# Three input buffers per chunk, wider zero products, and a rolled-up general path in a gated-recurrence and MLP kernel

## The chip, the cores and the metric

One core of one Trainium2 chip. The time is device microseconds of one execution; the kernel runs as one launch, and the host only lays the inputs out and the output back.

## The reference

Every head of `q`, `k`, `v`, `f_logit` (4 batches, 8 heads, 768 steps, 48 wide) runs a gated linear recurrence; the result, as 3072 tokens of 384, goes through a two-layer MLP (384 to 2048 to 384) with the activation h*tanh(softplus(h)). All is float32.

```python
f = 1.0 / (1.0 + np.exp(-f_logit))
for t in range(S):
    state = f[:, :, t, :, None] * state + np.einsum('bhd,bhe->bhde', k[:, :, t], v[:, :, t])
    y[:, :, t] = np.einsum('bhd,bhde->bhe', q[:, :, t], state)
...
x = np.ascontiguousarray(attn_out.transpose(0, 2, 1, 3)).reshape(B * S, H * D)
h = x @ w_in
sp = np.where(h > 20.0, h, np.log1p(np.exp(np.minimum(h, 20.0))))
g = h * np.tanh(sp)
return (g @ w_out).astype(np.float32)
```

## The kernel before

The recurrence is cut into 24 chunks (6 stretches of 128 steps for each of 4 batches). For a chunk n, `load` brings the inputs `l` (gate logits), `k`, `q`, `v` (256 KB each) into one of two buffers (`n % 2`); `prep` forms the cumulated gates on ScalarE (lines 358, 359, 374, 375), VectorE (357) and TensorE (362, chunks 0 to 7) and multiplies `k` and `q` by them (277, on VectorE or GpSimd); `attn0` makes the scores (398) and masks them (404); `attn1` transposes `k` (423, copied by 426); `attn2` forms the state's update (440; `mid` at 453 or 456, `tmp` at 458); `attn3` makes the chunk's output (474, 486), splits it into a high and a low part in `xt` (512, 517 or 519), moves the state on (502), and, when the last chunk of a group of four is done, spreads some rows of `xt` over the others by DMA (525).

Each group of four chunks is 512 tokens of the MLP, worked off as 16 units (one for each 128 hidden columns j): `moe_in` (219, nine products of 512 columns), the activation `mish` (229 to 237, over ScalarE, VectorE and GpSimd), `moe_out` (242, nine products). The first two groups take turns: j 0 to 7 of group 0, j 0 to 7 of group 1, then j 8 to 15 of each. Before the first unit of a j, `split_w(j)` loads 768 KB of weights (`raw`, two buffers, line 320) and makes a high and a low part: ScalarE 322 and 329, VectorE 324, 325, 327 and 330. Results leave through `ob` (585 to 591) by DMA (592).

All this is recorded first, as steps with a cost, and `Plan.order` sets each engine's order by list scheduling with those costs and with the buffers as dependences; the program is then issued in that order. All DMAs are issued by SyncE's queue (SP). Where the plan has TensorE idle before the first `moe_out`, `Plan.issue` puts products on zeros (`idle`, line 310) into the gap.

At the end, `ends` (the chunks' last decays) is tested (620 to 625) into `flag`; all five engines load `flag` (633) and jump over the body of `tc.If` (634), the general path for decays that the fast path can't take. It isn't run with these inputs, but its code lies between the branch and the end of the program.

Of the kernel before, what the change touches and what calls it, by code (L numbers as in the profile page):

```python
# [9 lines left out]
F32 = mybir.dt.float32  # L10
# [29 lines left out]
LEAD = [(-4, 4), (24, 32)]  # L40
LAG = 2


class Plan:
# [130 lines left out]
def recurrence_moe_kernel(  # L175
# [36 lines left out]
    state0 = ctile([P, P], F32, "state0")  # L212


    def moe_in(h, xt, j):
# [24 lines left out]
    def moe_out(o, m, gh, gl, j, first, last):  # L240
# [6 lines left out]
    with tc.tile_pool(name="work", bufs=1) as pool, tc.tile_pool(  # L247
# [5 lines left out]
        l_, k_, q_ = (ring(nm, 2, [P, NP, C]) for nm in "lkq")  # L253
        v_ = ring("v", 2, [P, H * 64])
# [54 lines left out]
        def idle():  # L309
            nc.tensor.matmul(zeros[:, 0:P], state0[:, 0:P], state0[:, 0:P], start=True, stop=True)  # L310
# [23 lines left out]
        def load(n, parts):  # L334
            i = n % 2
# [8 lines left out]
        def prep(n, parts):  # L344
            i = n % 2
# [40 lines left out]
        def attn0(n, parts):  # L386

            k, q = k_[n % 2], q_[n % 2]
# [18 lines left out]
            def reads(s):  # L407
                return pairs(("k", n % 2), range(s, s + st)) + pairs(("q", n % 2), range(s, s + st))
# [8 lines left out]
        def attn1(n):  # L417
            b, key = at1.rearrange("p (a c) -> p a c", a=NP), ("at", 2)
            k = k_[n % 2]
# [5 lines left out]
            add("pe", 400, transposes, pairs(("k", n % 2)), [key])  # L425
            add("act", T_ACT(GT, True), lambda: nc.scalar.activation(kt_s, b, AF.Copy), [key], ["kt"])

        def attn2(n):
            last = n >= NCH - B
            st, ks = state[:, n % B], ("st", n % B)  # L430
            v = v_[n % 2]
# [13 lines left out]
            if n >= GC:  # L445
                scores, mask, reads, writes = late[n]
                add("pe", 1208, lambda: [update(), scores()], ["kt", ("v", n % 2)] + reads,
                    list(dict.fromkeys(keys[: 2 - last] + writes)))
                mask()
            else:  # L450
                add("pe", 745, update, ["kt", ("v", n % 2)], keys[: 2 - last])
# [8 lines left out]
        def attn3(n):  # L460
            i = n % 2
# [99 lines left out]

        def out_unit(u):
# [18 lines left out]
            if last:  # L581
                dst = halves[g] if j < NF - 1 else out[:, g * GT : (g + 1) * GT]
                for m in range(NK):
# [6 lines left out]
                    else:  # L590
                        add("dve", T_DVE(GT), lambda m=m: nc.vector.tensor_copy(ob_[m], o_[m]), [("o", m)], pairs(("ob", m)))
# [4 lines left out]
        for u in range(len(units) + LAG):  # L596
# [22 lines left out]
        ok, oks = at1[0:1, 0:1], state.rearrange("p b a c -> p (b a c)")[:, : NCH * NP]  # L619
        add("dve", 119, lambda: nc.vector.tensor_scalar(  # L620
            oks, ends.rearrange("p n a b -> p (n a b)"), DEC_OK, None, ALU.is_ge),
            [x for n in range(NCH) for x in pairs(("end", n))], [("st", b) for b in range(B)])
        add("dve", 169, lambda: nc.vector.tensor_reduce(okc, oks, mybir.AxisListType.X, ALU.add), [("st", 0)], ["okc"])
        add("pe", 26, lambda: nc.tensor.matmul(ok, ones, okc, start=True, stop=True), ["okc"], [("at", 2)])
        add("dve", 65, lambda: nc.vector.tensor_copy(flag, ok), [("at", 2)], ["flag"])
# [8 lines left out]
    with tc.If(good < total):  # L634
        xs = dram.tile([DM, NT], F32, tag="xs", name="xs")
        with tc.tile_pool(name="slow", bufs=1) as pool, tc.tile_pool(
# [9 lines left out]
            with tc.For_i(0, B, 1) as b:  # L646
                for p in range(NP):
                    f, k, q = (st([P, NCB, C], nm) for nm in ("sf", "sk", "sq"))
                    for dst, src in ((f, fl), (k, kk), (q, qq)):
                        nc.sync.dma_start(  # L650
                            dst, src.rearrange("(c b) p a t -> p a c b t", b=B)[:, p, :, ds(b, 1), :]
                            .rearrange("p c b t -> p c (b t)"),
# [3 lines left out]
                    with tc.For_i(0, D, 1) as e:  # L656
                        v = st([P, S], "sv")
                        for i in range(2):
                            nc.sync.dma_start(
                                v[64 * i : 64 * i + 64, :],  # L660
                                vt[ds(b, 1), 2 * p + i, ds(e, 1), :]
                                .rearrange("a c t -> (a c) t")
# [12 lines left out]
                        for i in range(2):  # L675
                            nc.sync.dma_start(
# [101 lines left out]
```

## Time and profile before

| | us |
|---|---|
| median of 3 runs | 529.99 |
| lowest, highest | 527.87, 534.02 |
| profiled execution, time | 533.71 |
| profiled execution, span (first to last instruction) | 531.9 |
| TensorE, busy share of the span | 96% |
| VectorE, busy share | 70% |
| ScalarE, busy share | 78% |
| GpSimd, busy share | 30% |

Busy time of TensorE counts the products on zeros too, and its matmuls overlap, so its share doesn't tell how much of the span is useful work.

### The profile page before, as it was taken

To read this page: it belongs to the slowest core of one execution; us is meant where nothing else is said; L and a number is where in the kernel's file an instruction comes from. 1 tells how busy PE (TensorE), PEld (TensorE's weight loads), DVE (VectorE), ACT (ScalarE), POOL (GpSimd) and SP (SyncE) were. 2 spreads that over 40 slices of the span, in tenths; PEclk is the share of its full clock that TensorE was granted. 3 is DMA by queue.
4 is the path that set the end of the run, shared out by engine and by line. 5 is a ranking of instruction groups with operands and counts; after the bars stand their busy time and mean duration, and the time that the engine had idled before them with its cause. 6 is when DMAs were issued, how large, how long until landed. Compare 5 with 4: busy or idle time off the path is not lost.

```text
span 531.9 us, 13034 instructions
## 1 busy us (share of the span) xinstructions
PE 512.8 (96%) x5358; PEld 409.7 (77%) x5358; DVE 369.7 (70%) x588; ACT 415.4 (78%) x731; POOL 157.4 (30%) x134
## 2 busy tenths in 40 slices
PE   8899999999899999999999999999999999999993
PEld 7678777777677777787787777787787787778882
DVE  4478999899897887866576777567657563645451
ACT  6777988888789798878778788878878776778770
POOL 2231442334132322412322332413131222132320
PEclk9899999999899999999999999999999999999998
DMA  7597554344230443321212330112221000000001
GB/s 263 208 293 257 167 173 131 88 154 140 98 99 21 143 138 110 118 64 60 62 41 90 101 100 25 58 41 90 61 79 41 4 0 33 26 33 1 1 1 67
DMA packets 22629, 48.91 MB, mean 92 GB/s; under 512 B 2656, under 2 KB 3808, under 8 KB 22560
## 3 DMA queue, kind: packets, MB, share of 16 engines
q1 hardware_dynamic: 22560, 47.98, 28.1%
q8 instruction: 44, 0.72, 0.6%
q14 instruction: 25, 0.20, 0.1%
HBM read 39.32 MB, written 6.29 MB: 86 GB/s over the span
## 4 chain that ended last, share of the span: by engine, by line
PE 82%; DVE 7%; DMA 3%; ACT 3%; issue 2%; SPq 0%; POOL 0%; DVEq 0%; ACTq 0%
PE h L219 35%; PE o L242 34%; PE at L486 2%; PE at L474 2%; PE at L440 2%; DMA xt<-xt 2%; PE at L423 2%; PE at L398 2%; DVE wt L325 1%; DMA raw<-ww 1%; DVE g L232 1%; DVE wl L330 1%; DVE n L231 1%; PE at L362 1%; PE o L310 1%
## 5 line engine op out<-in xcount | busy, mean ns | idle before, releaser
L237 POOL TENSOR_TENSOR gl<-g,gh 128x512 fp32r<-128x512 f32 x96 | 129.9, 1356 | 302.5 <-ACT gh L236 274.3
L219 PE MATMUL h<-xt,wh 128*128 128x512 f32 x576 | 185.9, 404 | 3.4 <-DVE g L235 2.4
L219 PEld LDWEIGHTS h<-xt,wh 128*128 128x128 f32 x576 | 105.7, 189 | 31.1 <-DVE g L235 4.8
L242 PE MATMUL o<-gh,wh 128*128 128x512 f32 x288 | 116.5, 405 | 0.0
L219 PE MATMUL h<-xt,wl 128*128 128x512 f32 x288 | 114.2, 397 | 0.0
L242 PE MATMUL o<-gl,wh 128*128 128x512 f32 x288 | 113.7, 395 | 0.0
L242 PE MATMUL o<-gh,wl 128*128 128x512 f32 x288 | 113.7, 395 | 0.0
L231 DVE SCALAR_TENSOR_TENSOR n<-n 128x512 f32<-128x512 f32 x96 | 71.1, 740 | 54.7 <-ACT n L230 54.5
L235 DVE TENSOR_TENSOR g<-g,h 128x512 f32<-128x512 f32 x96 | 65.3, 682 | 42.1 <-ACT h L234 41.7
L229 ACT ACTIVATE n<-h,hcap 128x512 f32<-128x512 f32 x96 | 65.7, 685 | 31.5 <-PE h L219 30.8
L233 ACT ACTIVATE h<-n,two 128x512 f32<-128x512 f32 x96 | 65.8, 686 | 29.3 <-DVE g L232 29.3
L236 ACT ACTIVATE gh<-g 128x512 fp32r<-128x512 f32 x96 | 60.1, 627 | 16.1 <-DVE g L235 14.1
L232 DVE TENSOR_TENSOR g<-h,n 128x512 f32<-128x512 f32 x96 | 66.1, 689 | 8.9 <-POOL gl L237 1.1
L230 ACT ACTIVATE n<-n,hcap 128x512 f32<-128x512 f32 x96 | 69.2, 721 | 2.1
L219 PEld LDWEIGHTS h<-xt,wl 128*128 128x128 f32 x288 | 54.4, 189 | 13.3
L242 PEld LDWEIGHTS o<-gh,wh 128*128 128x128 f32 x288 | 54.0, 188 | 13.5 <-ACT ob L588 0.3
L242 PEld LDWEIGHTS o<-gl,wh 128*128 128x128 f32 x288 | 54.0, 187 | 13.3
L242 PEld LDWEIGHTS o<-gh,wl 128*128 128x128 f32 x288 | 54.1, 188 | 11.8
L234 ACT ACTIVATE h<-h 128x512 f32<-128x512 f32 x96 | 55.9, 582 | 1.8
L519 DVE TENSOR_TENSOR xt<-at,xt 128x256 fp32r<-128x256 f32 x40 | 15.9, 418 | 13.4 <-ACT xt L512 13.2
L502 POOL TENSOR_TENSOR state<-tmp,ends 128x256 f32<-128x256 f32 x20 | 16.7, 834 | 28.6 <-PE at L474 22.1
L404 DVE TENSOR_TENSOR a<-at,causal 128x256 f32<-128x256 f32 x44 | 17.7, 418 | 7.4 <-PE at L398 7.3
(102 smaller groups left out, 525.2 us busy)
## 6 DMA issues: line engine op xcount, KB each, us to landing
raw<-ww SPq DMA_DIRECT2D x16, 768.0 KB, 5.2
v<-vn SPq DMA_DIRECT2D x24, 256.0 KB, 3.7
k<-kk SPq DMA_DIRECT2D x23, 256.0 KB, 3.1
q<-qq SPq DMA_DIRECT2D x23, 256.0 KB, 2.9
out<-ob SPq DMA_DIRECT2D x18, 256.0 KB, 2.3
l<-fl SPq DMA_DIRECT2D x16, 256.0 KB, 2.7
xt<-xt SPq DMA_DIRECT2D x15, 128.0 KB, 2.1
l<-ft SPq DMA_DIRECT2D x7, 256.0 KB, 3.8
```

Of the source, the lines that this page charges most:

```text
L219: nc.tensor.matmul(h, w[:, j, a * P : (a + 1) * P], xt[:, x, a, :], start=(n == 0), stop=(n == 3 * NK - 1))
L229: ("act", T_ACT(GT, True, 1), 0, lambda: nc.scalar.activation(u, h, AF.Relu, bias=hcap, scale=-1.0)),
L230: ("act", T_ACT(GT, False, 1), 0, lambda: nc.scalar.activation(u, u, AF.Exp, bias=hcap, scale=-1.0)),
L231: ("dve", T_DVE(GT), 1, lambda: nc.vector.scalar_tensor_tensor(n, u, 2.0, u, ALU.add, ALU.mult)),
L232: ("dve", T_DVE(GT), 0, lambda: nc.vector.tensor_tensor(g, h, n, ALU.mult)),
L233: ("act", T_ACT(GT, False, 1), 0, lambda: nc.scalar.activation(h, n, AF.Ln, bias=two)),
L234: ("act", T_ACT(GT, True), 0, lambda: nc.scalar.activation(h, h, AF.Exp, scale=-1.0)),
L235: ("dve", T_DVE(GT), 0, lambda: nc.vector.tensor_tensor(g, g, h, ALU.mult)),
L236: ("act", T_ACT(GT), 0, lambda: nc.scalar.activation(gh, g, AF.Copy)),
L237: ("pool", T_POOL(GT), 1, lambda: nc.gpsimd.tensor_tensor(gl, g, gh.bitcast(F32), ALU.subtract)),
L242: nc.tensor.matmul(o, w[:, j, m * P : (m + 1) * P], x, start=(first and i == 0), stop=(last and i == 2))
L404: add("dve", T_DVE(NP * CH), lambda e=e: nc.vector.tensor_tensor(a_[e], sc[e], causal[:, None, :].broadcast_to([P, NP, CH]), ALU.mult), [k ...
```

## The change

Four edits. The rings of `l`, `k`, `q` and `v` get three buffers (`NR`) for two, which also removes dependences from the plan; the scheduler then writes another order for every engine. The zero product is 256 columns wide for 128, and is put in at twice the pitch, in gaps of over 527 ns of the plan for 313; the order holds 66 of the narrow ones before and 27 of the wide ones now. The test of `ends` is recorded ahead of the last unit's output, and the last copies into `ob` read `flag`, so that the test can't be put behind them. The general path becomes nested loops with fewer and wider DMAs, most of them issued by ScalarE's queue. Counted in the two built programs, waits included and a matrix product as its weight load and its multiply, the jump over it spans 746 instructions of TensorE before and 161 now, 284 and 163 of ScalarE, 250 and 139 of VectorE, 332 and 179 of SP, 175 and 125 of GpSimd. The scratch for dynamic DMAs is set to 1024. In the changed file everything behind line 41 stands one line lower, and more from line 560 on.

```diff
+NR = 3
...
-                    while at + 313.0 < self.start[i]:
+                    while at + 527.0 < self.start[i]:
                         self.idle()
-                        at += 213.0 if at > 6500.0 else 426.0
+                        at += 427.0 if at > 6500.0 else 853.0
...
-        l_, k_, q_ = (ring(nm, 2, [P, NP, C]) for nm in "lkq")
-        v_ = ring("v", 2, [P, H * 64])
+        l_, k_, q_ = (ring(nm, NR, [P, NP, C]) for nm in "lkq")
+        v_ = ring("v", NR, [P, H * 64])
...
-            nc.tensor.matmul(zeros[:, 0:P], state0[:, 0:P], state0[:, 0:P], start=True, stop=True)
+            nc.tensor.matmul(zeros[:, : 2 * P], state0[:, 0:P], state0, start=True, stop=True)
...
-            i = n % 2
+            i = n % NR
...
+        def check():
+            ok, oks = at1[0:1, 0:1], state.rearrange("p b a c -> p (b a c)")[:, : NCH * NP]
+            add("dve", 119, lambda: nc.vector.tensor_scalar(
...
+            add("dve", 65, lambda: nc.vector.tensor_copy(flag, ok), [("at", 2)], ["flag"])
...
-                        add("dve", T_DVE(GT), lambda m=m: nc.vector.tensor_copy(ob_[m], o_[m]), [("o", m)], pairs(("ob", m)))
+                        add("dve", T_DVE(GT), lambda m=m: nc.vector.tensor_copy(ob_[m], o_[m]),
+                            [("o", m)] + ["flag"] * (u == len(units) - 1), pairs(("ob", m)))
...
+            if u == len(units):
+                check()
             if u >= LAG:
                 out_unit(u - LAG)
...
-                for p in range(NP):
+                with tc.For_i(0, NP, 1) as p:
...
-                        nc.sync.dma_start(
+                        nc.scalar.dma_start(
...
-                for j in range(NF):
-                    moe_in(h, xt, j)
+                with tc.For_i(0, NF, 1) as j:
+                    for w, whole in zip(wj, (wh, wl)):
+                        nc.vector.tensor_copy(w, whole[:, ds(j, 1), :].bitcast(F32))
+                    moe_in(h, xt, 0, *(w[:, :, : NK * P] for w in wj))
...
-    nc = bacc.Bacc("TRN2", target_bir_lowering=False, num_devices=1)
+    nc = bacc.Bacc("TRN2", target_bir_lowering=False, num_devices=1, dynamic_dma_scratch_size=1024)
```

Three places in the order. First SP, at the start, behind the loads of chunks 0 and 1. Names are buffers: `l0` is the first buffer of `l`, `raw0` the first of the weights. Before the change SP issues here:

```order
L339 DMA l0_81<-ft 128x512
L320 DMA raw0_112<-ww 128x1536
L320 DMA raw1_113<-ww 128x1536
L339 DMA l1_82<-ft 128x512
L339 DMA k0_83<-kk 128x512
L339 DMA q0_85<-qq 128x512
L342 DMA v0_87<-vn 128x512
```

The same place now:

```order
L340 DMA l0_81<-ft 128x512
L340 DMA k2_86<-kk 128x512
L340 DMA q2_89<-qq 128x512
L343 DMA v2_92<-vn 128x512
L340 DMA l1_82<-ft 128x512
L321 DMA raw0_116<-ww 128x1536
L340 DMA k0_84<-kk 128x512
L321 DMA raw1_117<-ww 128x1536
```

The first two weight loads moved behind the inputs of chunk 2, which no longer wait for a buffer of chunk 0.

Second ScalarE, between chunk 2's `mid` and the output of chunk 3. Before the change, up to chunk 3's `mid` and the rest of chunk 2's output (`wt` holds weights on their way to `wh`):

```order
L453 ACTIVATE mid0_95<-at2_118 128x256
L358 ACTIVATE l0_81<-l0_81 128x512
L329 ACTIVATE wh_61<-wt0_114 128x768
L359 ACTIVATE l0_81<-l0_81,ones_69 128x512
L426 ACTIVATE kt0_89<-at2_118 128x512
L512 ACTIVATE xt0_97<-o1_122 128x2x128
L512 ACTIVATE xt0_97<-o0_121 128x2x128
L517 ACTIVATE xt0_97<-o1_122 128x2x128
L322 ACTIVATE wt0_114<-raw0_112 128x768
L453 ACTIVATE mid0_95<-at2_118 128x256
L329 ACTIVATE wh_61<-wt1_115 128x768
L517 ACTIVATE xt0_97<-o0_121 128x2x128
```

The same place now:

```order
L454 ACTIVATE mid0_99<-at2_122 128x256
L323 ACTIVATE wt0_118<-raw0_116 128x768
L323 ACTIVATE wt1_119<-raw1_117 128x768
L513 ACTIVATE xt0_101<-o1_126 128x2x128
L427 ACTIVATE kt0_93<-at2_122 128x512
L513 ACTIVATE xt0_101<-o0_125 128x2x128
L518 ACTIVATE xt0_101<-o1_126 128x2x128
L518 ACTIVATE xt0_101<-o0_125 128x2x128
L454 ACTIVATE mid0_99<-at2_122 128x256
L330 ACTIVATE wh_61<-wt0_118 128x768
```

Before, the copy of the third weight load (322) stood ahead of chunk 3's `mid` and the first two had been copied earlier; now the first two stand here, and the third behind the output of chunk 3.

Third SP, at the end, from the last group's output on. Before the change SP issues the three output DMAs first:

```order
L592 DMA out<-ob_109 128x512
L592 DMA out<-ob_110 128x512
L592 DMA out<-ob_111 128x512
L633 TENSOR_LOAD flag
L633 ISA x2
L634 COMPARE_AND_BRANCH
```

The same place now:

```order
L639 TENSOR_LOAD flag
L639 ISA x2
L604 DMA out<-ob_113 128x512
L604 DMA out<-ob_114 128x512
L604 DMA out<-ob_115 128x512
L640 COMPARE_AND_BRANCH
```

The load of `flag` and its two checks moved ahead of the last three output DMAs.

## Rows read from the trace of the kernel before

**Rows 1.** The page: its span, and the chain of waits that ended last, by engine.

```profile
span 531.9 us, 13034 instructions
...
PE 82%; DVE 7%; DMA 3%; ACT 3%; issue 2%; SPq 0%; POOL 0%; DVEq 0%; ACTq 0%
```

**Rows 2.** Busy time by stretch: start and end, length, then busy us (and instructions) of PE, PEld, DVE, ACT and POOL, the granted clock, the DMA share and GB/s. The row for 44.4 to 160 is of VectorE alone.

```profile
20.00:44.40 24.40, 22.40 (x493) 19.42 (x491) 18.93 (x30) 17.72 (x39) 6.79 (x6) 0.95 0.74 238
60.00:130.00 70.00, 68.96 (x734) 54.16 (x735) 65.17 (x94) 60.46 (x102) 27.34 (x20) 1.00 0.43 138
130.00:139.00 9.00, 6.65 (x21) 4.71 (x20) 8.35 (x10) 5.97 (x9) 2.63 (x2) 0.81 0.29 89
160.00:442.80 282.80, 282.80 (x3166) 224.11 (x3165) 198.70 (x330) 228.34 (x408) 82.99 (x68) 1.00 0.22 68
...
44.40:160.00 115.60, 107.13 (x152) 0.99 0.44 142
```

**Rows 3.** The timeline of the start: start and length in us, engine, line, operation, tiles, count, and in brackets the idle time before it and what ended it.

```profile
18.09 0.57 PE L440 MATMUL at<-v,kt 64*64 64x64 f32 x22 [2.57 <-issue]
19.83 0.55 DVE L324 TENSOR_SCALAR wt<-wt 128x768 int32<-128x768 int32 x1
26.15 0.38 ACT L453 ACTIVATE mid<-at 128x256 f32<-128x256 f32 x1
31.54 0.89 ACT L322 ACTIVATE wt<-raw 128x768 f32<-128x768 f32 x1 [1.53 <-DMA raw<-ww]
32.33 0.37 ACT L453 ACTIVATE mid<-at 128x256 f32<-128x256 f32 x1
37.37 0.54 SPq L320 DMA_DIRECT2D raw<-ww  x1
38.44 1.48 SPq L525 DMA_DIRECT2D xt<-xt  x2
44.39 0.73 PE L219 MATMUL h<-xt,wh 128*128 128x512 f32 x2 [0.86 <-DMA xt<-xt]
```

**Rows 4.** What VectorE waited for from 40 to 160 us: line, releaser, us in total, times, longest.

```profile
DVE g L235 <- ACT h L234: 2.9, 3, 1.8
DVE xt L519 <- ACT xt L512: 2.0, 3, 0.8
DVE wt L324 <- ACT wt L322: 1.2, 2, 1.0
DVE n L231 <- ACT n L230: 1.0, 2, 0.5
```

**Rows 5.** The products on zeros, all of them (duration min/median/max in ns, first and last start), and, from the timeline of TensorE, the stop near 133 us and the products behind it.

```profile
L310 PE MATMUL o<-state x132: 271/275/580, 1.1 to 55.1; 128*128 128x128 f32 x132
...
132.60 0.40 PE L219 MATMUL h<-xt,wl 128*128 128x512 f32 x1
135.13 1.22 PE L219 MATMUL h<-xt,wh 128*128 128x512 f32 x2 [2.13 <-DVE g L235]
...
138.85 0.39 PE L242 MATMUL o<-gh,wh 128*128 128x512 f32 x1
```

**Rows 6.** The end, from the timeline.

```profile
522.09 1.74 SPq L592 DMA_DIRECT2D out<-ob  x3
522.77 0.69 DVE L591 COPY ob<-o 128x512 f32<-128x512 f32 x1 [0.71 <-PE o L242]
523.38 0.14 DVE L625 CAST flag<-at 1x1 int32<-1x1 f32 x1
```

**Rows 7.** Lines 633, 634 and, for SyncE alone, 773 (the program's last instructions): queue, operation, count, duration min/median/max in ns, first and last start in us.

```profile
L633 SPq TENSOR_LOAD <-flag x1: 491/491/491, 523.9 to 523.9; - x1
...
L634 PEldq COMPARE_BRANCH  x1: 3542/3542/3542, 524.4 to 524.4; - x1
L634 SPq COMPARE_BRANCH  x1: 50/50/50, 524.7 to 524.7; - x1
L634 DVEq COMPARE_BRANCH  x1: 72/72/72, 524.4 to 524.4; - x1
...
L634 POOLq EVENT_SEMAPHORE  x1: 17/17/17, 524.9 to 524.9; - x1
...
L634 DVEq EVENT_SEMAPHORE  x1: 21/21/21, 528.6 to 528.6; - x1
L634 SPq EVENT_SEMAPHORE  x8: 17/17/17, 528.6 to 529.1; - x8
...
L773 SPq EVENT_SEMAPHORE  x5: 28/28/28, 529.2 to 529.5; - x5
...
L773 SPq EVENT_SEMAPHORE  x5: 17/28/28, 530.8 to 531.8; - x5
```

**Rows 8.** DMA: the instruction queues over the whole span (packets, MB, share), the same from 524.5 us to the end, and the output's DMAs (count, KB, median us to landing).

```profile
q8 instruction: 44, 0.72, 0.6%
q14 instruction: 25, 0.20, 0.1%
...
q14 instruction: 8, 0.07, 3.0%
q8 instruction: 2, 0.03, 2.2%
...
out<-ob SPq DMA_DIRECT2D x18, 256.0 KB, 2.3
```

More of the change, by code (lines that the diff above doesn't have):

```diff
@@ L238, in mish, with moe_out @@
         )
-    def moe_out(o, m, gh, gl, j, first, last):
+    def moe_out(o, m, gh, gl, j, first, last, woh=woh, wol=wol):
         for i, (w, x) in enumerate(((woh, gh), (wol, gh), (woh, gl))):
@@ L407, in reads @@
             def reads(s):
-                return pairs(("k", n % 2), range(s, s + st)) + pairs(("q", n % 2), range(s, s + st))
+                return pairs(("k", n % NR), range(s, s + st)) + pairs(("q", n % NR), range(s, s + st))
             if n >= GC:
@@ L450, in attn2 @@
             else:
-                add("pe", 745, update, ["kt", ("v", n % 2)], keys[: 2 - last])
+                add("pe", 745, update, ["kt", ("v", n % NR)], keys[: 2 - last])
             if n < B:
@@ L560, in recurrence_moe_kernel @@
             attend()
+        def check():
+            ok, oks = at1[0:1, 0:1], state.rearrange("p b a c -> p (b a c)")[:, : NCH * NP]
+            add("dve", 119, lambda: nc.vector.tensor_scalar(
+                oks, ends.rearrange("p n a b -> p (n a b)"), DEC_OK, None, ALU.is_ge),
+                [x for n in range(NCH) for x in pairs(("end", n))], [("st", b) for b in range(B)])
+            add("dve", 169, lambda: nc.vector.tensor_reduce(okc, oks, mybir.AxisListType.X, ALU.add), [("st", 0)], ["okc"])
+            add("pe", 26, lambda: nc.tensor.matmul(ok, ones, okc, start=True, stop=True), ["okc"], [("at", 2)])
+            add("dve", 65, lambda: nc.vector.tensor_copy(flag, ok), [("at", 2)], ["flag"])
         def out_unit(u):
@@ L615, in recurrence_moe_kernel @@
                 attend()
+            if u == len(units):
+                check()
             if u >= LAG:
                 out_unit(u - LAG)
[L619 to L625, printed above, removed]
         plan.idle = idle
@@ L684, in recurrence_moe_kernel @@
                 tok = ds(g * GT, GT)
-                for a in range(NK):
-                    for e in range(2):
-                        r, hd = 64 * e, head_at(a, e)
-                        for m in range(3):
-                            nc.sync.dma_start(
-                                x[r + m : r + 64 : 4, a, :], xs[hd * D + m : (hd + 1) * D : 3, tok]
-                            )
-                        r0 = head_at(NP - 1, e) * D
-                        nc.sync.dma_start(x[r + 3 : r + 64 : 4, a, :], xs[r0 + a : r0 + D : 3, tok])
+                rows = xs.rearrange("(a e r m) t -> a e m r t", e=2, r=D // 3, m=3)
+                for e in range(2):
+                    for m in range(4):
+                        src = rows[:NK, e, m, :, tok] if m < 3 else rows[NP - 1, e, :, :, tok]
+                        nc.scalar.dma_start(x[64 * e + m : 64 * e + 64 : 4], src.rearrange("a r t -> r a t"))
                 xt = pool.tile([P, 2, NK, GT], F32R, tag="sxt", name="sxt")
```

54 lines of the change are left out of this document (28 added, 26 removed).

## The prediction

> **What bounds the kernel now.** I read the chain of waits first, then busy time by stretch, then the timeline of the start, then the last ten microseconds. The chain runs through TensorE for 82% of the span [rows 1]. By stretch, TensorE is busy without a break from 160 to 443 us [rows 2], and the zero products end at 55.1 us [rows 5], so that time is useful work: the change alters no instruction count there and can take nothing from it. What is left are three places. (1) The start: the MLP's first product waits until 44.39 us, last for a DMA of `xt` [rows 3]; TensorE fills waits with zeros. (2) From 44.4 to 160 us VectorE is busy for 107.1 of 115.6 us [rows 2], and at 132.6 us TensorE stops for 2.13 us for VectorE's line 235 and then runs at a mean granted clock of 0.81 [rows 2, 5]. Here the two engines bound each other: TensorE is busy for 68.96 of 70 us from 60 to 130. (3) The end: the last copy into `ob` starts at 522.77 us, and the span ends at 531.9 [rows 1, 6]. I make the sum against the profiled execution, 533.7 us, which lies 3.7 above the median of the runs shown; the difference goes onto the median.
>
> **The end.** SP issues the last output DMA until 522.09 + 1.74 = 523.83 us [rows 6], loads the flag from 523.9, and branches at 524.7 [rows 7]. In the new order load and checks stand ahead of these DMAs, the flag being ready long before (the decays' last reader is chunk 23). So SP branches at 523.85: 0.9 us earlier. VectorE still loads behind its last copy; it saves at most the same.
>
> Behind the branch SP's next instruction runs at 528.6, 3.9 us later; VectorE needs 4.2 us, TensorE's branch itself 3.5; GpSimd only 0.5 [rows 7]. In that stretch the instruction queues bring in 8 and 2 pieces [rows 8]: code has to be fetched for four engines and not for GpSimd. The jumps span 250 to 746 instructions on those four and 175 on GpSimd; now they span 125 to 179. That is between the two ends, none paid and all paid, and far nearer to GpSimd's 175. But a piece is 8 KB for the engines besides TensorE (0.20 MB in 25), and 16 KB for TensorE (0.72 MB in 44) [rows 8]; TensorE's 44 pieces carry its 10,716 products and weight loads, some 67 bytes each, so 8 KB are about 122 instructions. If the piece that holds the branch and the next one are present, a jump of d lands inside from (244 - d) of 122 starting places: 86% for VectorE's 139, 66% for ScalarE's 163, 53% for SP's 179, all of TensorE's. All three land with 0.86 x 0.66 x 0.53 = 30%. So I take it that one stays out, SP the likeliest, and since the last instructions wait for every engine, one costs nearly what four did: 0 gained here, with 2.3 more as the other bound. (That bound: with no fetch, the end waits for the last output, issued by 523.83 and landing 2.3 us later [rows 8], 526.1; SP's run from 528.6 to 531.85 without its gap, below, is 2.0 us, and some of its waits pass earlier; the end is then near 527.5, which is 4.4 us under 531.9, and 2.1 of these are counted here anyway.)
>
> The page "Runtime: NRT & Kernel Launch" of the Trainium skill, section "Instruction fetch mechanics", says that two pages of 256 instructions are held and that only a jump out of them is fetched. By that every jump of the new program would land, and the third case below would be the forecast. The trace differs on the piece: 8 KB, not 16, for four engines.
>
> One more gap: between SP's instructions at 529.5 and 530.8 there is 1.3 us with nothing [rows 7], where its neighbours are 0.07 apart; I read it as the next piece, fetched late. SP has 22 instructions behind its landing place, so a boundary falls among them with 22/122 = 18%; I count the gap as gone, -1.2, with 0 as the other bound. **Sum of the end: -0.9 - 1.2 = -2.1**, between -0.5 and -4.4.
>
> **The start, for TensorE.** Before, ScalarE stood at line 322 for the third weight load (1.53 us and 0.89 for the copy) with chunk 3's `mid` behind it, which ran at 32.33 [rows 3]. Now the third load's copy is behind chunk 3's output. From `mid` of chunk 2 (26.15, nothing on its way is removed) I add the new order: two weight copies of 0.89, four halves of `xt` and chunk 3's `kt`, so that chunk 3's `mid` comes near 30.3 and the last `xt` part near 34. SP must issue the fourth weight load before that DMA, and it waits for the second split on VectorE, by the next paragraph near 33.9; so the DMA goes out near 34 for 38.44, again with a weight load just ahead of it (37.37 before [rows 3]). With the same 5.9 us to the first product it starts near 40: **-4.4** for TensorE.
>
> **The start, for VectorE.** The same edit puts the first two weight loads behind the inputs of chunk 2. VectorE began its first weight split at 19.83 [rows 3]; now the copy ahead of it ends near 26.5 + 0.9 = 27.4, so it begins 7.6 us later. Part of that is recovered, since VectorE was busy for only 18.93 of 24.4 us from 20 to 44.4 [rows 2]. Following the new order through with about 0.95 us for a pass over 768 columns, VectorE has two splits less one pass done at 41 us where it had three and a bit: some 1.5 us of work behind. From there it is the busier of the two until 160 us, and all its work up to the last split is the same. So TensorE's lead of 4.4 us counts only as far as VectorE can follow: it waited 7.1 us from 40 to 160 on the four largest lines, 2.9 for ScalarE's line 234, 2.0 for `xt`, 1.2 for weights, 1.0 for 230 [rows 4], and none of these waits is for a chunk's input. The bounds are +1.5 (nothing recovered) and -4.4 (the lead is kept). I take **-1.0**, nearer to the first, because at 93% busy there is little to recover.
>
> **Third buffers elsewhere.** In the stretches behind 160 us no wait of TensorE is left to remove; cost and gain 0.
>
> **Zero products.** 66 become 27, twice as wide. They run in waits, so the work that hides them is the wait itself. A wide one can hold up ready work for one product: 2 x 0.275 us before [rows 5], so at most about 0.3 us more each, of which only the few in front of ready work count: +1 as a bound. Fewer instructions also move the place at which TensorE stood for 2.57 us with nothing to wait for (18.09, rows 3) by eight products, not enough to hide it; if it goes, -2.6. If the sparser zeros leave a stop like the one at 132.6, the clock falls to 1.2 GHz again: there nine products took 138.85 - 135.13 = 3.7 us [rows 5] where nine take 2.1 at 2.4 GHz, so +1.6. I take 0 for all.
>
> **Sum.** 533.7 - 2.1 - 1.0 = 530.6 for an execution like the profiled one; on the median, 530.0 - 3.1 = **526.9**. A measurement of this kernel can tell about 1%, 5.3 us, from no change.
>
> **Rivals.**
> - *The lead is kept.* VectorE's waits vanish with the earlier start, and TensorE ends 4.4 us earlier in front: 530.0 - 4.4 - 2.1 = 523.5. For it: 7.1 us of waits [rows 4]. Against: 93% busy.
> - *All jumps land.* The end gives 4.4 with the front at -1.0: 524.6. For it: GpSimd's 175 landed. Against: SP's 179 needs a favourable starting place.
> - *Slower: the late weight splits.* VectorE's first split begins 7.6 us later and it recovers nothing, because in the new order the waits for chunk 2 and 3 stay ahead of the splits: 530.0 + 7.6 - 2.1 = 535.5. It decides from the point where VectorE idles more than 5.5 + 4 us between 20 and 44 us. For it: VectorE bounds until 160 us. Against: its idle time there gives room for most of it.
> - *The change doesn't do what it says.* The fetch of code remains and the flag is loaded late all the same, the start moves by nothing: 530. I count it into the forecast's own spread.
>
> **How the numbers follow.** Forecast 45%, lead kept 20%, all jumps land 23%, slower 12%. The forecast's own range, from its bounds (-4.4 to +1.5 in front, -0.5 to -2.1 at the end, +1 for zeros), is 523.5 to 532. Lowest is the lead kept with all jumps landing, 521.2, with the 2.57 us stop gone 518.6; highest the slower case. Leaving out no more than 2 in 10: 519.5 to 533. Faster by over 1%, below 524.7: most of "lead kept" (0.16), half of "all jumps land" (0.12), a little of the forecast (0.06): 0.34. Slower by over 1%, above 535.3: half of the slower case and a bit, 0.08. Within 1%: 0.58.
>
> **What would show it.** Line 220's first product near 40 us; VectorE's first line 325 near 27, and no less than 92% busy from 45 to 150; TensorE stopping in that stretch for VectorE for more than the 2.13 us of before; line 640's branch on SP 0.9 us closer to the last copy, and its first instruction behind either 3.9 or 0.5 us later; no gap in SP's last run. I am wrong if the first split isn't late, or if a stop of TensorE behind 160 us appears, where I count on none.

## The result, and the profile after

The changed kernel takes 535.94 us (median of 17 runs, 533.30 to 538.28) where the kernel before takes 531.93 in the same comparison: a ratio of 1.0078, 95% interval 1.0058 to 1.0098. It is slower by 4.0 us, less than 1% but well outside the uncertainty of the ratio. I had forecast 526.9 us and a range of 519.5 to 533.0.

The profiled execution took 535.56 us. From its page, the span and the chain by engine, against [rows 1]:

```profile
span 533.7 us, 12867 instructions
...
PE 76%; DVE 13%; ACT 6%; issue 3%; DMA 1%; DVEq 0%; ACTq 0%; SPq 0%
```

VectorE's part of the chain grew from 7 to 13% and TensorE's fell from 82 to 76. The end was better than forecast: the last copy into `ob` starts at 527.69, 6.0 us ahead of the span's end (9.1 before, [rows 1, 6]). So in front of that copy the changed kernel's profile is 527.69 - 522.77 = 4.9 us behind, where I had it gain 1.0. These are two single executions, and that of before was 1.8 us over its median. By the medians the loss in front is larger: 4.0 us slower with an end some 3 us shorter makes about 7. The run with the end alone (below), whose order in front is that of before, says the same: its last copy starts at 520.24, 7.5 us ahead of the changed kernel's.

The start went the way of the forecast. From the timeline of the start of the changed kernel, columns as in [rows 3]:

```profile
27.36 0.56 DVE L325 TENSOR_SCALAR wt<-wt 128x768 int32<-128x768 int32 x1
...
31.32 0.39 ACT L454 ACTIVATE mid<-at 128x256 f32<-128x256 f32 x1 [0.51 <-PE at L441]
...
35.20 1.89 SPq L526 DMA_DIRECT2D xt<-xt  x3
...
41.73 0.72 PE L220 MATMUL h<-xt,wh 128*128 128x512 f32 x2
```

VectorE's first weight split is at 27.36 (19.83 before), and the MLP's first product at 41.73 (44.39), 2.7 us earlier and not 4.4. Even these 2.7 aren't all the change's: in three other profiles with the order of before (the end alone, two buffers, the aligned end below) that product starts at 42.19, 44.16 and 43.49. The loss comes later. Busy time by stretch of 20 us, columns as in [rows 2]:

```profile
100.00:120.00 20.00, 17.86 (x131) 13.97 (x130) 18.67 (x27) 17.39 (x29) 5.42 (x4) 0.91 0.40 133
120.00:140.00 20.00, 19.62 (x159) 15.31 (x158) 18.57 (x25) 14.77 (x25) 6.72 (x5) 1.00 0.40 139
140.00:160.00 20.00, 16.66 (x70) 12.52 (x69) 17.79 (x24) 16.51 (x27) 5.82 (x4) 1.00 0.27 86
160.00:180.00 20.00, 19.11 (x136) 15.02 (x138) 17.40 (x23) 18.85 (x35) 6.57 (x4) 1.00 0.09 26
```

And the stops of TensorE in the same stretch, from its timeline:

```profile
102.75 0.73 PE L220 MATMUL h<-xt,wh 128*128 128x512 f32 x2 [2.14 <-DVE g L236]
127.70 0.74 PE L220 MATMUL h<-xt,wh 128*128 128x512 f32 x2 [0.38 <-DVE g L236]
143.46 0.73 PE L220 MATMUL h<-xt,wh 128*128 128x512 f32 x2 [1.45 <-DVE g L236]
152.35 0.73 PE L220 MATMUL h<-xt,wh 128*128 128x512 f32 x2 [0.23 <-DVE g L236]
156.37 0.73 PE L220 MATMUL h<-xt,wh 128*128 128x512 f32 x2 [1.66 <-DVE g L236]
165.92 0.73 PE L220 MATMUL h<-xt,wh 128*128 128x512 f32 x2 [0.89 <-DVE g L236]
```

Where there were two such stops, of 0.22 and 2.13 us (the longer in [rows 5]), there are six, all behind the last multiplication of a unit's activation on VectorE (line 236, the last reader of the buffer `h` that TensorE writes next). A single number for this is the busy row from 80 to 180 us, of the kernel before and then of the changed one:

```profile
80.00:180.00 100.00, 97.47 (x808) 75.74 (x806) 90.61 (x125) 84.31 (x140) 31.55 (x22) 0.98 0.32 102
```

```profile
80.00:180.00 100.00, 92.54 (x701) 71.41 (x704) 91.04 (x122) 83.69 (x140) 31.70 (x22) 0.98 0.32 107
```

TensorE idles for 2.5 us of these 100 before and for 7.5 after. The last zero product starts at 52.5 us, so this is missing useful work. To place all of the 4.9 us I took, for each unit's first product, the useful products ahead of it in the program's order off its time (0.234 us for one of line 220, 0.238 for 243, the small ones fitted the same way where TensorE never idles). By that estimate, against the profile of before, the changed kernel is ahead by some 3 us at 50, by 1.5 to 2 at 80 (as the small products are fitted), behind by 3.8 at 180 and by 4.8 at 450 us: of the 6 to 7 us that it lost behind 80, all but 1.0 fell before 180. The idle time from 80 to 180 serves below as the mark of an order.

### The profile page after: what moved, and what is told of

Same layout as the page of the kernel before. It is cut to its first block, busy times and chain, and to the rows that moved or that the text cites. A ratio compares the mean times of both kernels' runs of the same rounds, so it can differ in the third digit from the quotient of the medians.

```text
span 533.7 us, 12867 instructions
## 1 busy us (share of the span) xinstructions
PE 511.1 (96%) x5280; PEld 403.0 (76%) x5280; DVE 372.6 (70%) x588; ACT 414.9 (78%) x731; POOL 158.0 (30%) x134
## 4 chain that ended last, share of the span: by engine, by line
PE 76%; DVE 13%; ACT 6%; issue 3%; DMA 1%; DVEq 0%; ACTq 0%; SPq 0%
PE h L220 32%; PE o L243 32%; DVE wt L328 2%; PE at L487 2%; PE at L475 2%; PE at L441 2%; DVE n L232 2%; DVE wt L326 2%; PE at L424 2%; PE at L399 2%; DVE g L236 1%; DVE g L233 1%; DVE wl L331 1%; DMA raw<-ww 1%; ACT n L231 1%
## 5 line engine op out<-in xcount | busy, mean ns | idle before, releaser
L237 ACT ACTIVATE gh<-g 128x512 fp32r<-128x512 f32 x96 | 60.3, 628 | 21.9 <-DVE g L236 19.4
L441 PEld LDWEIGHTS at<-v,kt 64*64 64x64 f32 x704 | 13.5, 134 | 11.8 <-issue 5.2
```

The costliest lines, as they stand in the source:

```text
L237: ("act", T_ACT(GT), 0, lambda: nc.scalar.activation(gh, g, AF.Copy)),
L441: nc.tensor.matmul(u[c][half(e), p, :], kt_s[half(c), p, half(e)], v[half(c), c0 : c0 + 64], start=True, stop=True)
```

## The experiments

Ratios are to the kernel before, timed in turn on the same chip. The groups of runs were on different chips, so only the ratios are compared across them.

**What each part does.** Three runs on the changed kernel with parts taken back. With `NR` at 2 the planner's order is again that of before, row by row, up to the last outputs.

```diff
-NR = 3
+NR = 2
...
-            nc.tensor.matmul(zeros[:, : 2 * P], state0[:, 0:P], state0, start=True, stop=True)
+            nc.tensor.matmul(zeros[:, 0:P], state0[:, 0:P], state0[:, 0:P], start=True, stop=True)
```

Both edits (the second with the narrow pitch): 

> The changed kernel with two buffers and the narrow zero products of before: each engine's order up to the last outputs is that of before, and only the end is new (flag ahead of the last copies, rolled-up general path). In the two profiles the span goes on for 9.1 us from the start of the last copy into ob before and for 6.0 us after. Theory A (the end saves, the order of the third buffers costs): 3.1 us under the kernel before, a ratio of 0.994, and the front as in [rows 3]. Rival B (the shorter stretch behind the last copy is only shifted waiting, since the copy itself came later): no difference to before, 1.000.

Measured: 0.9934 (0.9901 to 0.9967). First edit alone: 

> As the run with the end alone, with the wide zero products too: the changed kernel less the third buffers. Theory A: within 0.2% of the run with the end alone, 0.994 of before, since the zeros run in waits. Rival C (the sparser, wider zeros cost: held-up work, a stop that lowers the granted clock): as the changed kernel, 1.008 of before, with a stretch of granted clock under 0.95 between 80 and 180 us that the run with the end alone lacks.

Measured: 0.9938 (0.9914 to 0.9962). Second alone: 

> The changed kernel with the narrow zero products of before; order of all engines besides the zeros as in the changed kernel. Theory A: as the changed kernel, 1.008 of before within 0.2%, with VectorE's first weight split near 27 us and stops of TensorE for VectorE behind 80 us. Rival C: 0.994 of before or less.

Measured: 1.0038 (1.0009 to 1.0067), first split at 27.6 us, 6.7 us of stops for line 236 from 80 to 180. So the end gains some 3.5 us; with two buffers the zeros do nothing; what costs comes with the third buffers and the order that the planner writes for them. Whether the narrow zeros give back 0.4% beside three buffers stays open: the intervals of 1.0038 and 1.0078 overlap, and the last copies of the two profiles are at 527.6 and 527.7.

**The end.** How the branch and what follows it look in the changed kernel, columns as in [rows 7]:

```profile
L640 SPq EVENT_SEMAPHORE  x8: 17/17/17, 531.8 to 532.3; - x8
...
L640 ACTq COMPARE_BRANCH  x1: 50/50/50, 527.5 to 527.5; - x1
...
L640 ACTq EVENT_SEMAPHORE  x1: 17/17/17, 528.0 to 528.0; - x1
L640 DVEq COMPARE_BRANCH  x1: 72/72/72, 528.6 to 528.6; - x1
L640 SPq COMPARE_BRANCH  x1: 50/50/50, 528.8 to 528.8; - x1
L640 DVEq EVENT_SEMAPHORE  x1: 21/21/21, 532.1 to 532.1; - x1
```

ScalarE is over its jump in 0.5 us; SP stands 3.0 and VectorE 3.5. To tell a fetch from the length of the jump, I moved the code and left the jumps as long as they were:

```diff
             if u == len(units):
                 check()
+                add("sp", 10, lambda: nc.sync.addr_align(256, offset=16, max_nops=0), ["flag"])
+                add("dve", 10, lambda: nc.vector.addr_align(256, offset=16, max_nops=0), ["flag"])
```

> The run with the end alone (two buffers, narrow zeros, new end), with one directive each on SP and VectorE behind the last use of the test: the code that follows is loaded from slot 16 of a block of 256 instruction slots on, with a branch over the padding. SP's jump of 179 then starts near slot 26 and VectorE's of 139 near slot 78, so that both land in the same block of 256 or in the next 128. In the run with the end alone SP stands 2.95 us behind its branch and VectorE 3.5, while ScalarE stands 0.45. Theory F (these are two fetches of code, which depend on where the jump starts and not on its length alone): both come down to about 0.5 us, and the end comes 1.6 to 2.4 us earlier than with the end alone, held then by the landing of the last output: a ratio of 0.989 to 0.991 to before. Rival G (the stand is the jump itself or the wait for other engines): 0.994 as the end alone, the stands of 3 us remain.

Measured: 0.9915 (0.9888 to 0.9941). The rows of its branch:

```profile
L642 SPq EVENT_SEMAPHORE  x8: 17/17/17, 523.9 to 525.9; - x8
...
L642 DVEq COMPARE_BRANCH  x1: 67/67/67, 523.3 to 523.3; - x1
L642 SPq COMPARE_BRANCH  x1: 55/55/55, 523.5 to 523.5; - x1
L642 DVEq EVENT_SEMAPHORE  x1: 21/21/21, 523.8 to 523.8; - x1
```

Both stands are some 0.5 us now: theory F holds, the 3 us were the place of the code. The instruction queue q14 [rows 8] brings in 3 pieces from 523.2 us on, where in the changed kernel it brings 5 from 528.5 on. Its size was a miss: from the last copy to the end it is 4.9 us against 6.0 with the end alone, 1.0 us gained and not 1.6 to 2.4. SP's eight rows tell why: they no longer run in half a microsecond but from 523.9 to 525.9, since now they wait for the last outputs, issued until 523.4 and 2.7 us on their way at the median in that profile; the last of them lands at 525.77. The ratios alone (0.9915 and 0.9934) don't separate the two kernels.

**Is it the late weight splits?** That was the rival whose time (535.5) the measurement hit. Theory A1 first: the first two weight loads ahead of chunk 2, three buffers kept.

```diff
         while done < 4 * GC:
+            if done == 8:
+                split_w(0)
+                split_w(1)
             attend()
...
-                        (), pairs((nm, i), range(s, s + st)), 65.5 * st)
+                        [("raw", 0), ("raw", 1)] if n == 2 else (), pairs((nm, i), range(s, s + st)), 65.5 * st)
```

> The changed kernel with the first two weight loads recorded ahead of chunk 2 and the loads of chunk 2 made to depend on them in the plan, so that the plan puts them ahead of chunk 2 as before the change; third buffers, wide zeros and new end stay. Theory A1 (it is the late first splits): VectorE's first split starts near 20 us instead of 27.4, the stops of TensorE for VectorE between 80 and 180 us shrink, and the time is that of the run with the end alone, 0.994 of before, or up to 2.7 us lower where the earlier first product is kept. Rival A2 (the cause is the plan's new order as a whole, in the units behind 80 us): no nearer to 0.994 than to the changed kernel's 1.008, wherever the first split starts.

Measured: 0.9942 (0.9914 to 0.9970); first split at 14.3 us. The time is theory A1's, but that run has another order throughout. With the aligned end added to it: 

> The changed kernel with the first two weight loads ahead of chunk 2 (as in the run with early weights, 0.994 of before) and with the aligned end of the run before this one. Theory F: 1.6 to 2.4 us under the run with early weights, 0.990 of before; rival G: 0.994.

Measured: 0.9957 (0.9931 to 0.9983). The profile has 4.8 us from the last copy to the end for 6.2, but the times show no gain over 0.9942; a miss.

The next pair takes VectorE's work away (it leaves out line 328) and keeps every engine's order:

```diff
             add("dve", T_DVE(W_TILE), lambda: nc.vector.scalar_tensor_tensor(
-                t, high, -(2**31), t, ALU.bitwise_and, ALU.bitwise_or), [kr], [kt], port=True)
+            add("dve", T_DVE(W_TILE), lambda: None, [kr], [kt], port=True)
```

> The changed kernel with line 328 left out, VectorE's third pass over each weight tile (the sign bits, so the low parts are of other numbers); the order of all engines stays. VectorE then has 16 passes of 1.19 us, 19 us, less to do between 27 and 160 us. Theory V (VectorE's late start on the splits takes TensorE's lead and more): the stops of TensorE for VectorE's line 236 (7.0 us from 40 to 200) shrink to under 2 us, the last copy comes at least 5 us earlier than in the changed kernel, and the kernel is level with the run with the end alone that leaves out the same, or under it by up to the 2.7 us by which its first product is earlier. Rival O (the new order holds TensorE through another engine or through transfers): it stays over 3 us above that run.

Measured: 0.9995 (0.9974 to 1.0017). 

> The run with the end alone with line 328 left out in the same way: the measure for the run before this one. In the order of before TensorE waits 2.4 us for line 236 between 40 and 200 us and loses some 1.6 us to a lower granted clock near 133 us. Theory V: these go, 2 to 4 us under the run with the end alone, 0.987 to 0.990 of before. Rival O: 0.994, nothing changes, since VectorE doesn't bound.

Measured: 0.9934 (0.9898 to 0.9969). TensorE's waits for line 236 from 40 to 200 us in the first of the two (us, times, longest; 7.0 in 7 in the changed kernel):

```profile
PE h L220 <- DVE g L236: 5.3, 7, 1.4
```

And from 80 to 180 us in the second, where the kernel before had 2.4 in 2:

```profile
PE h L220 <- DVE g L236: 2.5, 2, 2.1
```

So 19 us less of VectorE's work give the changed order 4.4 us back and the order of before nothing; its stop of 2.1 us stays. The first kernel remains 3.2 us above the second, which is rival O's number, but not its mechanism: TensorE still waits for VectorE's line 236. Theory V is right for a part only. VectorE's load isn't all. The sharper test takes away only the backlog at the start:

```diff
-            add("dve", 469, lambda: nc.vector.tensor_scalar(t, t, 3, None, ALU.logical_shift_left), (), [kt], port=True)
-            add("dve", T_DVE(W_TILE), lambda: nc.vector.scalar_tensor_tensor(
+            add("dve", 469, lambda: j < 2 or nc.vector.tensor_scalar(t, t, 3, None, ALU.logical_shift_left), (), [kt], port=True)
+            add("dve", T_DVE(W_TILE), lambda: j < 2 or nc.vector.scalar_tensor_tensor(
```

(the same for line 328) 

> The changed kernel with VectorE's lines 325, 326 and 328 left out for the first two weight tiles only (their low parts are of other numbers); the order of all engines stays. That is 2 x (0.55 + 0.95 to 1.13 + 0.95), some 5 us of VectorE's work between 27 and 37 us, in the place where the changed order falls behind. Theory L (the backlog of the late first splits is carried through to 160 us): with 5 us less of it the whole loss goes: stops of TensorE for line 236 between 40 and 200 us under 3 us (7.0 in the changed kernel), a ratio of 0.996 to 0.999 to before, 5 to 6 us under the changed kernel. Rival I (what costs is where the new order puts weight passes and activation passes in VectorE's queue behind 90 us): the stops at 103, 143, 156 and 166 us stay, 5 us or more together, and the gain is under 3 us, 1.002 to 1.008.

Measured: 1.0057 (1.0030 to 1.0083). Its busy row from 80 to 180 us, then TensorE's largest wait in that stretch (line and releaser, us, times, longest):

```profile
80.00:180.00 100.00, 92.24 (x707) 71.24 (x706) 90.55 (x123) 83.44 (x140) 30.70 (x22) 0.98 0.33 107
```

```profile
PE h L220 <- DVE g L236: 6.7, 6, 2.1
```

The idle time is 7.8 us (7.5 in the changed kernel). Theory L falls: the work that the late first splits leave on VectorE is not what costs. The order written around the late splits stays in this run.

**Other orders with three buffers.** The third buffer only from chunk 4 on, and the first weight loads recorded elsewhere but not forced:

```diff
+def slot(n):
+    return n % 2 if n < GC else (n - GC) % NR
```

> The changed kernel with the third buffer only from chunk 4 on: chunks 0 to 3 take two buffers in turn, chunk 4 on three. The planner writes a third order of its own, whose start has the first weight loads ahead of chunk 2's inputs except the first gate logits, as before the change. Theory L: first split near 20 us, ratio 0.994 as with two buffers. Rival I: the time follows the order that the planner happens to write behind 90 us, so it can land anywhere from 0.990 to 1.010, with TensorE's stops for line 236 going along with it.

Measured: 1.0039 (1.0005 to 1.0072), first split at 19.2 us: early splits, and slow all the same. 

> The changed kernel with only the place changed at which the first two weight loads are recorded (behind chunk 1 instead of behind chunk 3), without a dependence: three buffers, wide zeros and new end. The planner keeps them behind chunk 2's inputs in SyncE's order, so the first splits stay late (near 26 us), but the order behind is another one. Theory L: as the changed kernel, 1.004 to 1.010. Rival I: another time than the changed kernel's, by more than 0.4%, though the first split is as late.

Measured: 1.0032 (1.0003 to 1.0061), first split at 25.5. The first speaks against theory L. The second does so only weakly, since its interval reaches into theory L's range. Rival I, that the time goes with the order as a whole, is left; with a range from 0.990 to 1.010 it could hardly have failed here.

**Is it the passes in front of line 236?** In the changed kernel's stop at 102.75 VectorE's queue holds weight passes (328 and 325) directly ahead of line 236. I moved these, and every weight pass in such a place (some sixty rows), behind it when the order is written out:

```diff
+        for i in [i for i in reversed(order) if i in self.passes]:
+            p = q = order.index(i)
+            for n in range(p + 1, count):
+                j = order[n]
+                if i in self.steps[j][3] or self.start[j] > self.start[i] + 3000.0:
+                    break
+                if j in self.ends:
+                    q = n
+                    break
+            order.insert(q, order.pop(p))
```

> The changed kernel in which, when the plan's order is written out, each of VectorE's weight passes (lines 325, 326, 328, 331) moves behind the next line 236 if that is planned within 3 us and nothing in between needs the pass; some sixty rows of VectorE's order change place, and no other engine's order changes. Theory I (weight passes in front of line 236 hold TensorE): the stops of TensorE for line 236 between 40 and 200 us fall from 7.0 to under 4 us, and the time by 2 to 5 us, a ratio of 0.998 to 1.004. Rival R (something else in the new order costs, and the stops move elsewhere): within 0.2% of the changed kernel, 1.006 to 1.010.

Measured: 1.0324 (1.0281 to 1.0368). 

> The aligned end on the order of before (two buffers, narrow zeros), with the same rule for VectorE's weight passes. That order has 2.4 us of stops for line 236. Theory I: these and the lower granted clock near 133 us go at best, 0 to 3 us under the run with the aligned end (0.9915 of before), 0.986 to 0.992. Rival R: 0.9915 or, where moved passes make weights late, up to 0.995.

Measured: 1.0153 (1.0102 to 1.0204). 

> As the first of these three, but the weight passes move behind the last of the activation's three VectorE lines (232, 233, 236) of any unit that is planned within 3 us. Theory I: at least the gain of the first run, unless weights come late: then TensorE's line 220 waits for line 331 or 328 instead, and the gain is given back. Rival R: within 0.2% of the changed kernel.

Measured: 1.0400 (1.0356 to 1.0444). All three miss, in the other direction. The first of them, its busy row from 80 to 180 us and TensorE's largest wait there:

```profile
80.00:180.00 100.00, 86.62 (x622) 64.76 (x620) 83.28 (x112) 74.81 (x122) 28.99 (x21) 0.98 0.32 105
```

```profile
PE h L232 <- DVE g L248: 12.7, 9, 2.8
```

(lines stand 12 lower there.) VectorE is busy for 83.3 us and not 91.0. In that stretch it now waits 11.7 us for the input that ScalarE's line 235 makes for line 236, where it waited 2.1. So the sixty passes as a whole filled time in which VectorE would have stood, and moving them all is no cure. What the few ahead of the six stops cost, these runs don't tell. The changed kernel's own timeline tells some of it. The unit that TensorE waits for at 102.75:

```profile
96.07 0.71 ACT L231 ACTIVATE n<-n,hcap 128x512 f32<-128x512 f32 x1
...
98.68 0.68 DVE L232 SCALAR_TENSOR_TENSOR n<-n 128x512 f32<-128x512 f32 x1
...
101.39 0.58 ACT L235 ACTIVATE h<-h 128x512 f32<-128x512 f32 x1
...
102.00 0.69 DVE L236 TENSOR_TENSOR g<-g,h 128x512 f32<-128x512 f32 x1
```

Line 236 begins 0.03 us behind the end of line 235, its input, so the two passes ahead of it held up nothing. The unit had lost 1.9 us before: line 231 was done at 96.78, and line 232 waited on VectorE behind line 326, a weight pass of 2.06 us. At the six stops line 236 begins 0.03, 0.16, 0.38, 0.32, 1.41 and 0.90 us behind the end of line 235. So what stands directly ahead of line 236 accounts for 3.1 us of the 6.75 at most. That form of theory I holds for less than half of the stops.

**Is it three buffers at all?** The planner writes a new order whenever anything in its input changes. So I changed something that changes no instruction. First the place at which the first weight loads are recorded, with two buffers: 

> The run with the end alone (two buffers, 0.9934 of before) with only the place changed at which the first two weight loads are recorded, as in the run with another plan of three buffers. Theory S (the order that the planner writes is a draw, and a new draw moves the time by some tenths of a per cent to one per cent either way): another time than 0.9934, by more than 0.4%, with TensorE's loss between 80 and 180 us going along. Theory T (three buffers are the cause): within 0.4% of 0.9934.

Measured: 0.9985 (0.9957 to 1.0013). That is 0.5% above the run with the end alone, as theory S says, but only just clear of noise: the two intervals overlap. Then one number of the planner's, with two and with three buffers:

```diff
 def T_POOL(n):
-    return n * 2.3 + 60
+    return n * 2.4 + 60
```

> The run with the end alone with one number of the planner's changed, GpSimd's cost per column from 2.3 to 2.4 ns, which changes no instruction, only their order. Theory S: another time than 0.9934, by more than 0.4%. Theory T: within 0.4%.

Measured: 0.9901 (0.9865 to 0.9937). That is 0.3% from 0.9934, within theory T's 0.4%. It is 0.8% from the run just before, with intervals apart: two orders with two buffers do differ. 

> The changed kernel (three buffers, 1.0078) with the same one number of the planner's changed. Theory S: another time by more than 0.4%, and it may come under 1.000. Theory T: 1.002 or more.

Measured: 0.9913 (0.9883 to 0.9944). This is the changed kernel, with the same instructions in another order (and zeros where that order has gaps), and it is 1.6% faster than it. Its busy row from 80 to 180 us and TensorE's wait for line 236 there:

```profile
80.00:180.00 100.00, 98.38 (x821) 76.96 (x820) 92.40 (x134) 87.84 (x148) 32.16 (x25) 1.00 0.36 118
```

```profile
PE h L220 <- DVE g L236: 0.7, 3, 0.4
```

1.6 us of idle time where the changed kernel has 7.5. Theory T falls here: the order costs, and not three buffers as such. That the order is a mere draw, as theory S has it, is less sure. The new number is also the truer one: for line 238's 512 columns the planner reckons 1289 ns with 2.4 and 1238 with 2.3, and the median measured in the changed kernel is 1299. Both orders planned with it are the fastest of the table, and no run tells a better plan from a lucky one. All orders with the new end, by that mark (100 us less TensorE's busy time there) and by the start of VectorE's first weight split:

| order | buffers | TensorE idle from 80 to 180 us | first split, us | ratio |
|---|---|---|---|---|
| GpSimd's cost at 2.4 | 2 | 2.7 | 14.2 | 0.9901 |
| GpSimd's cost at 2.4 | 3 | 1.6 | 16.2 | 0.9913 |
| that of before | 2 | 2.4 | 18.8 | 0.9934 |
| early weights | 3 | 1.8 | 14.3 | 0.9942 |
| weights recorded elsewhere | 2 | 3.6 | 19.4 | 0.9985 |
| weights recorded elsewhere | 3 | 3.7 | 25.5 | 1.0032 |
| third buffer from chunk 4 on | 3 | 4.5 | 19.2 | 1.0039 |
| the changed kernel's | 3 | 7.5 | 27.4 | 1.0078 |

The mark and the ratio rise together; in the first four rows, where little idle time is left in the stretch, it no longer sorts them. It sees only its stretch: the fastest order also has the earliest first product (39.15 us). The first splits go along with the ratio too, so the table alone doesn't rule them out. Against them stand two runs: the one without their work on VectorE (1.0057), and the third buffer from chunk 4 on, which splits as early as the kernel before and is slow.

**Both gains in one kernel.** 

> Two buffers, narrow zeros, the new end with both jumps aligned, and GpSimd's cost per column in the planner at 2.4 ns. Theories F and S: from the last copy to the end 4.9 us as in the run with the aligned end (6.0 without), in front the order of the run with that cost: 1.0 us under that run, 0.988 of before. If the gains don't add up: 0.990.

Measured: 526.13 us, 0.9914 (0.9889 to 0.9938). From the last copy to the end it is 4.9 us as hoped, but the time is no lower than without the alignment (0.9901): the gains are not shown to add up. It beats both kernels, as the runs at 0.9901, 0.9913 and 0.9915 do.

## Why the prediction was wrong

- *The end, -2.1: right in mechanism, 1.0 short.* The end is 3.1 us shorter. SP's branch is 1.1 us behind the start of the last copy and was 2.0: the 0.9 of the flag. SP's last run has no gap: it takes 1.2 us where it took 2.6, about the 1.2 forecast. The rows of line 781, against [rows 7]:

```profile
L781 SPq EVENT_SEMAPHORE  x10: 17/28/28, 532.4 to 533.6; - x10
```

  The term that was mis-sized is "one costs nearly what four did: 0 gained here": SP's stand fell from 3.9 to 3.0 us, a further 0.9. And two engines stay out, not one. By the counted lengths it could not be said which: VectorE's jump, the shortest of the three at 139, had been given 86% to land. The bound with all landing, 2.3 more, measured 1.0.
- *The start for TensorE, -4.4: 2.7.* Chunk 3's `mid` came at 31.3 and not 30.3, the last `xt` part was sent from 35.2 and not 34, and from there it took 6.5 us to the first product where I had kept the 5.9 of before. As said, other profiles of the old order have the first product up to 2.2 us earlier than the one I started from.
- *The start for VectorE.* First split forecast at 27.4, measured at 27.36; busy from 45 to 150 for 98.1 of 105 us, 93%, as said. This part was right, and beside the point: the run without these splits' backlog (1.0057) isn't shown to be faster. The 0.95 us for a pass was too low: in the kernel before, its three lines over 768 columns (325, 327 and 330) took 1.12, 1.09 and 1.27 us on the mean.
- *The step that failed* is what I did with it: "From there it is the busier of the two until 160 us, and all its work up to the last split is the same", with "The bounds are +1.5 (nothing recovered) and -4.4 (the lead is kept)". The work is the same, its order is not. The term of -1.0 for the front came out at 4.9 us of loss between the two profiles, and at about 7 by the medians, outside both bounds. I followed the new order to 45 us and carried the order of before from there to the end, though the diff hands the planner another set of dependences and it writes another order for all engines up to 180 us and beyond. That is where four further stops came in, and TensorE's wait for line 236 from 80 to 180 us rose from 2.4 to 6.8 us; the forecast put nothing there for it, and behind 160 us "cost and gain 0", where a stop of 0.89 us at 165.9 is one of the signs I had named against me. Bounds for that term had to take in a new order: the eight above, all with the new end, go from 0.9901 to 1.0078, some 9 us.
- *The rivals.* The late splits gave 535.5 and the measurement 535.9; the run without their work on VectorE shows that it wasn't by that mechanism, and a hit on the number is not a hit on the cause. The lead was there in part (2.7 us at most) and eaten between 50 and 180. All jumps landing didn't happen in the changed kernel.
- *Zeros, 0:* right with two buffers, open at 0.4% with three.

What stays open: which rows of the changed order make the difference between 1.6 and 7.5 us of idle time. Some 4.4 us of the loss answer to VectorE's load; it is not the work of the first splits on VectorE, and what stands directly in front of line 236 makes 3.1 us at most. Whether the order's late splits cost by another way than VectorE's work stays open too. Nor do eight orders settle whether three buffers are worse on the mean (three of five lie above 1.003, none of three with two buffers); that they need not be is shown by the 0.9913.

## What to carry to other kernels

Where a planner sets the order, an edit that changes its input is two edits: what it says, and a new order; here 1.8% lie between the best and the worst of eight, more than the edit moved the time. Before a gain or a loss is put down to the edit, change something in the planner that changes no instruction, with and without the edit, and compare the spreads; several such changes are better than one, since one can also be a truer cost. A forecast must carry that spread in its range where, as here, two engines hold each other up. For a branch at the end, look at the stand behind the branch engine by engine: here the place of the code decided it, with the jump's length unchanged.

## What the runs showed of the hardware that I had not expected

- *A stand behind a branch is a matter of place.* With the same lengths of jump (179 and 139 instructions) SP stood 3.0 us and then 0.5, VectorE 3.5 and then 0.5, after the code was moved. The page "Runtime: NRT & Kernel Launch" of the Trainium skill, section "Instruction fetch mechanics", says that a taken branch has its target fetched first if that isn't in the current window of two pages. The runs agree with that: one place of the code has the stand, another hasn't. They don't agree with the size of 256 instructions that the page gives for a block: by that, jumps of 139 and 179 would have landed from every place.
- *A VectorE pass can take twice as long beside GpSimd.* My sum used 0.95 us for a pass; in the changed kernel line 326 takes 0.96 at the median, 1.22 on the mean and 2.08 at most. From its timeline near 96 us:

```profile
95.83 0.95 DVE L331 TENSOR_TENSOR wl<-wt,wh 128x768 fp32r<-128x768 f32 x1
...
96.25 1.69 POOL L238 TENSOR_TENSOR gl<-g,gh 128x512 fp32r<-128x512 f32 x1 [2.50 <-ACT gh L237]
96.70 2.06 DVE L326 SCALAR_TENSOR_TENSOR wt<-raw,wt 128x768 int32<-128x768 int32 x1
```

  Line 326 begins 0.45 us behind GpSimd's line 238 and takes 2.06 us: the 1.24 until GpSimd is done, and 0.8. Line 331, of the same size, takes 0.95; it ends 0.5 us behind the start of line 238 and isn't held up. The Trainium skill's page "SBUF — State Buffer", section "SBUF: two separate sides", has the port that GpSimd shares with a VectorE instruction of two SBUF inputs (as line 326 is) as a lock: whoever starts first holds it for the whole instruction. This trace agrees.
- *Not every stop of TensorE lowers its clock.* From 100 to 120 us, with the stop of 2.14 us, the granted clock was 0.91; from 140 to 160, with stops of 1.45, 0.23 and 1.66, it was 1.00. What decides isn't shown.
